# Spreading sums of squares by a block-of-ones matmul, with one full-width Abs_reciprocal_sqrt pass and the norm's gain folded into two weights

## The chip, the cores and the metric

The kernel runs on one core of a Trainium2 chip. The metric is the time of one execution on the device in microseconds; less is better. Before the change it is 224.84 us, the median of two runs (224.73 and 224.95).

A core has five engines, each working through its own queue of instructions in order: TensorE (PE: matmuls; its weight loads, PEld, overlap them), VectorE (DVE), ScalarE (ACT), GpSimd (POOL) and SyncE (SP). POOL and SP here mostly issue transfers, which 16 DMA engines carry out. Matmul results go to PSUM, everything else lies in SBUF. Engines wait for each other by semaphores.

## The reference

Linear attention per head with an RMS norm over the 64 elements of a head, followed by an RWKV channel mix over the 512 columns that 8 heads make (8 batches, 576 rows each):

```python
def _attn_ref(q, k, v, g_norm):                    # (8, 8, 576, 64)
    kv = np.einsum('bhsd,bhse->bhde', k, v)
    out = np.einsum('bhsd,bhde->bhse', q, kv)
    rms = np.sqrt(np.mean(out * out, axis=-1, keepdims=True) + 1e-06)
    return (out / rms * g_norm).astype(np.float32)

def _moe_ref(x, mu_k, mu_r, w_k, w_v, w_r):        # x: (8, 576, 512)
    x_prev = np.concatenate([np.zeros((B, 1, D)), x[:, :-1, :]], axis=1)
    xk = mu_k * x + (1.0 - mu_k) * x_prev
    xr = mu_r * x + (1.0 - mu_r) * x_prev
    k = np.maximum(xk @ w_k, 0.0)                  # w_k: (512, 1024)
    v = k * k @ w_v                                # w_v: (1024, 512)
    r = 1.0 / (1.0 + np.exp(-(xr @ w_r)))          # w_r: (512, 512)
    return (r * v).astype(np.float32)
```

The gain `g_norm` has 64 elements, the same for every head.

## The kernel before, in words

**Layout.** Heads are taken in pairs, so that a pair fills 128 partitions (64 rows of one head, 64 of the other): 4 pairs per batch. q, k and v come from memory as float32 and are cast to bf16 by the loading DMA, one transfer of 590 KB for each of them and each batch, all issued by POOL (L294) in one queue; batch 0 is loaded in three parts. The weights (L283) are in the same queue: w_r and w_k behind batch 0, w_v behind batch 1.

**Attention of one batch** (`attention_part`), by piece name:
- `kv`: 48 small matmuls k^T v (L361), copied to SBUF by ACT or DVE (`kv copy`).
- `qT`: q transposed, on PE with copies out of PSUM (L391) for batches 0 to 3, by a DMA transpose from SP (L380) for batches 4 to 7.
- `u`: four matmuls per pair (L411), copied to uT by ACT or DVE (`u copy`), then squared on DVE (`u sq`, L420).
- `st`: 16 matmuls per batch against `sel`, a table of single ones (L440), which collect the sums of squares in few PSUM rows, packed so that 144 columns hold all pairs. ACT takes Ln and then Exp with factor -0.5 over these 144 columns (`rs`, L445 and L446): 1/rms.
- `rr`: 16 matmuls per batch of `selg` with `rs` (L463), which spread 1/rms back to a head's 64 rows, in PSUM.
- `x`: DVE forms uT times g (a column of `mu_sb`) times the spread 1/rms (L471), reading uT from SBUF and the factor from PSUM.
- `d`, `t`, `xk`, `xr`: shifted differences and the two blends (L488 to L507), written to rings that hold four batches.

**The mix** works on groups g of 512 rows, nine in all, whose borders are not those of the batches (576 rows). Each has K (32 matmuls of 512 columns, L548, with relu on ACT and its square on DVE), R (16, L571, sigmoid on ACT) and V (32, L591, times the sigmoid on DVE, then stores from SP). V of one group uses the squares of its own K.

**What sets the order.** Nothing at run time. The class `Planner` takes pieces with an engine (or a choice of two), an assumed duration, dependencies, buffers of rings of fixed depth and a due time, plays a schedule, and emits the instructions of each engine in the order found. Ring depths matter here: two buffers each of k, v, q, qT, kv, uT; two PSUM buffers of each of the kinds `at` (attention) and `mm` (mix). A load (`load k 3`) is emitted for POOL once the buffer of two batches before is done with: k and v after that batch's `kv`, q after its `qT`. The planner prices a 590 KB load at 0.36 us times 8 heads. It fills PE's planned gaps with dummy matmuls on zeros (L620), up to a planned time of 80 us. Changing any duration can change every order.

Act tables: sigmoid needs one set of ScalarE tables, Ln and Exp another (`ln_table`, L228); each change is one load of 1.28 us in the trace.

Of the kernel before, what the change touches and what calls it, by code (L numbers as in the profile page):

```python
# [8 lines left out]
FP32 = mybir.dt.float32  # L9
BF16 = mybir.dt.bfloat16  # L10
AF = mybir.ActivationFunctionType
ALU = mybir.AluOpType
# [24 lines left out]
class Planner:  # L37
# [40 lines left out]
    def run(self, warm=None):  # L78


        free, order, queue, dma, modes = {}, [], [], 0.0, {"PE": None, "ACT": "ln"}
        while self.left:
            best = {}
            for p in self.left:
# [14 lines left out]
                _, t, eng = min(ways)  # L99
# [51 lines left out]
def kernel(  # L151
# [13 lines left out]
    nc = tc.nc  # L165

    B, H, S, HD = q.shape
# [4 lines left out]
    NJ = 6  # L172
    NP = S // NJ
    HS = S // 2
    SEC = S // 4
    NI = NJ // 2
    G = 512
    NG = B * S // G
# [16 lines left out]
        "ln": (2, (128, SEC), FP32),  # L195
        "rs": (2, (128, SEC), BF16),
# [28 lines left out]

    table = [None]

    def ln_table():  # L228
        if table[0] != "ln":
            nc.scalar.preload_act_table_set("natural_log_exp_and_others")  # L230
            table[0] = "ln"


    ident = const.tile([128, 128], BF16, name="ident")
# [5 lines left out]
    eps = const.tile([128, 1], FP32, name="eps")  # L240
    zeros = const.tile([128, 512], BF16, name="zeros")
    sel = const.tile([128, NHP, 32], BF16, name="sel")
    selg = const.tile([128, NHP, NHP, 2, HD], BF16, name="selg")
# [6 lines left out]

    def consts_small(_):
        nc.vector.memset(zeros, 0.0)
        nc.vector.memset(eps, 1e-6)
        ln_table()
# [5 lines left out]
        nc.vector.memset(sel, 0.0)  # L260
        for e in range(2):
            for s in range(NHP):
                nc.vector.memset(sel[64 * e:64 * e + 64, s, 2 * s + e:2 * s + e + 1], 1.0)

    def consts_idents(_):
        make_identity(nc, ident)
# [6 lines left out]
        nc.tensor.matmul(ps, mu_raw, ident9, start=True, stop=True)  # L273
        nc.vector.tensor_copy(out=mu_sb, in_=ps)

    def consts_selg(_):

        for tl in range(NHP):
            rows = ident[:, 32 * tl:32 * tl + 2 * NHP].rearrange("p (s e) -> p s e", e=2)
            nc.scalar.copy(out=selg[:, tl], in_=rows.unsqueeze(3).broadcast_to([128, NHP, 2, HD]))  # L280

    def load_w(dst, src):
        nc.gpsimd.dma_start(out=dst, in_=src.rearrange("(c p) n -> p c n", p=128))  # L283
# [8 lines left out]
    def load(b, n, h0, h1, due):  # L292
        def fn(_):
            nc.gpsimd.dma_start(  # L294
                out=get(kvq[(n, b)])[:, h0:h1, :],
                in_=src[n][b, h0:h1].rearrange("h (p j) d -> p h (j d)", j=NJ),
            )

        p = add(f"load {n} {b}", {"POOL": 0.8}, fn, bufs=[kvq[(n, b)]], due=due, land=(h1 - h0) * 0.36)
        for h in range(h0, h1):  # L300
            loaded[(n, b, h)] = p
# [10 lines left out]
    p_selg = add("selg", {"ACT": 2.4}, consts_selg, deps=[p_ident], due=-800)  # L312
    p_wr = add("load w_r", {"POOL": 0.8}, lambda _: load_w(w_r_sb, moe_w_r), due=-700, land=2.6)
    p_wk = add("load w_k", {"POOL": 0.8}, lambda _: load_w(w_k_sb, moe_w_k), due=-699, land=5.2)
    for n in ("k", "v", "q"):
        load(1, n, 0, H, -698)
    p_wv = add("load w_v", {"POOL": 0.8}, lambda _: load_w(w_v_sb, moe_w_v), due=-697, land=5.2)
    for b in range(2, B):
        for n in ("k", "v", "q"):
# [19 lines left out]
    def attention_part(b, part, bufs, ps_buf):  # L339
# [5 lines left out]
        ln, rs = Buf("ln"), Buf("rs")  # L345

        def due(x):
            return 20 * b - 2 * x - 4 if b else -100 - x
# [79 lines left out]
                           due=due(20)))  # L428


        def place(i, s):
            return NHP // n * i + s // n, s % n

        pst = ps_buf()

        def st_mm(_):
            for s in range(NHP):
                for i, hp in enumerate(hps):
                    tl, sub = place(i, s)
                    nc.tensor.matmul(get(pst)[32 * tl:32 * tl + 32, 0, 0:SEC], sel[:, sub],  # L440
                                     sq.t[:, hp, SEC * s:SEC * s + SEC], start=(sub == 0), stop=(sub == n - 1))

        def st_ln(_):
            ln_table()
            nc.scalar.activation(out=get(ln), in_=pst.t[:, 0, 0:SEC], func=AF.Ln, bias=eps, scale=1.0 / HD)  # L445
            nc.scalar.activation(out=get(rs), in_=ln.t, func=AF.Exp, scale=-0.5)  # L446

        m = add(f"st {b}", {"PE": 0.3}, st_mm, mode=2, deps=sqs, bufs=[pst, sq, ln, rs], due=due(18))
        st = add(f"rs {b}", {"ACT": 0.74}, st_ln, deps=[m], bufs=[pst, ln, rs], due=due(17), mode="ln")


        xms = []
        step = min(2, n)
        for hp1 in range(hp0, hp0 + n, step):
            for half in range(2):
                cs = slice(HS * half, HS * half + HS)
                xs = slice(NP + HS * half, NP + HS * half + HS)

                def rr_mm(_, hp1, half, ps):
                    for i in range(step):  # L460
                        for c in range(2):
                            tl, sub = place(hp1 - hp0 + i, 2 * half + c)
                            nc.tensor.matmul(get(ps)[:, i, SEC * c:SEC * c + SEC],  # L463
                                             selg[:, tl, sub].rearrange("p e d -> p (e d)"), rs.t,
                                             start=True, stop=True)

                def x_mul(_, hp1, cs, xs, ps):
                    if xT.t is None:
                        nc.vector.memset(get(xT)[:, :, 0:1], 0.0)
                    hs = slice(hp1, hp1 + step)  # L470
                    nc.vector.scalar_tensor_tensor(  # L471
                        out=xT.t[:, hs, xs], in0=get(uT)[:, hs].rearrange("q h i jj p -> q h (i jj p)")[:, :, cs],
                        scalar=g_col, in1=ps.t[:, 0:step, 0:HS], op0=ALU.mult, op1=ALU.mult)

                ps = ps_buf()
                m = add(f"rr {b}", {"PE": 0.13 * step}, lambda _, hp1=hp1, half=half, ps=ps: rr_mm(_, hp1, half, ps),
                        deps=[st, p_selg], bufs=[ps, rs, xT], due=due(14))
                xms.append(add(f"x {b}", {"DVE": 0.15 + 0.3 * step},
                               lambda _, hp1=hp1, cs=cs, xs=xs, ps=ps: x_mul(_, hp1, cs, xs, ps),
                               deps=[m, p_mu] + [us[hp1 + i] for i in range(step)], bufs=[ps, uT, xT],  # L480
                               due=due(13)))
        last_rr[b] = m


# [43 lines left out]
            row += cnt  # L528


    p_first = add("first", {"PE": 0.01}, lambda _: None, deps=x_ready[0]["r"] + [p_wr], bufs=[warm], due=-1)
    hold = add("hold", {"PE": 0.01}, lambda _: None, bufs=[warm], due=-2000)

    def mix(g):
# [23 lines left out]
        for f2 in range(NFC // 2):  # L558
            ps, rt, u = Buf("mm"), Buf("relu"), k0 + 2 * f2
            ms = []  # L560
            for x in range(2):
                ms.append(add(f"K {g}", {"PE": 0.865}, lambda _, fc=2 * f2 + x, ps=ps: k_mm(_, fc, ps),
                              deps=ms or need["k"] + [p_wk], bufs=[ps, sqk], due=u + x))
            a = add(f"relu {g}", {"ACT": 1.04}, lambda _, ps=ps, rt=rt: k_relu(_, ps, rt), deps=ms[1:], bufs=[ps, rt], due=u + 2)
            sqs.append(add(f"sqk {g}", {"DVE": 0.7}, lambda _, f2=f2, rt=rt: k_sq(_, f2, rt), deps=[a], bufs=[rt, sqk], due=u + 4))

# [86 lines left out]
```

## Time and profile before

| | us |
|---|---|
| median of the runs | 224.84 |
| span of the profiled execution | 222.2 |
| PE busy in it | 205.6 |
| of which K, V and R (L548, L591, L571) | 165.9 |
| of which dummy matmuls L620 | 15.3 |
| VectorE busy | 144.8 |
| ScalarE busy | 124.1 |
| DMA engines full until about | 111 |
| last matmul ends | 218.0 |

The groups that the change touches (line, engine, operation, output<-inputs, shapes, count, then busy us and mean ns of one, then the idle time of the engine before them and its releaser):

```profile
L471 DVE SCALAR_TENSOR_TENSOR xT<-uT,mu_sb,at 128x576 bf16<-128x576 bf16 x29 | 22.6, 810 | 3.0 <-PE at L463 2.7
L420 DVE TENSOR_TENSOR sq<-uT 128x576 bf16<-128x576 bf16 x32 | 13.3, 454 | 0.8 <-ACT uT L221 0.7
L463 PE MATMUL at<-rs,selg 128*128 128x144 bf16 x120 | 11.1, 226 | 0.7 <-DVE xT L471 0.7
L440 PE MATMUL at<-sq,sel 128*32 128x144 bf16 x128 | 3.8, 229 | 0.2
L445 ACT ACTIVATE ln<-at,eps 128x144 f32<-128x144 f32 x10 | 3.8, 379 | 5.5 <-PE at L440 5.4
L446 ACT ACTIVATE rs<-ln 128x144 bf16<-128x144 f32 x10 | 3.2, 323 | 0.3
```

How to read it: the busy time of a group is the time in which at least one of its instructions was under way; matmuls overlap, so 120 of 226 ns fill only 11.1 us. The idle time behind the last bar is that of the engine just before the group, with what ended it.

### The profile page before, as it was taken

Reading aid. Unit: us, or ns where it says so; the run is one execution under the profiler, and the core shown is the slowest. Engines: PE = TensorE matmul, PEld = TensorE weight load, DVE = VectorE, ACT = ScalarE, POOL = GpSimd, SP = SyncE. Lnnn points to the kernel's source line nnn. Section 1 sums busy time; section 2 is a strip of 40 time slices with the busy share of each in tenths; the row PEclk is TensorE's granted clock in tenths of the full one; section 3 lists DMA queues with packets and bytes.
Section 4 is the critical chain, followed back from the end, with each engine's and each line's share of the span. In section 5 each row is a group of like instructions: output and inputs, shape, how many; then the busy total and the mean of one; then the engine's idle time right before and its main releaser. Section 6 shows DMA issues by size and latency. Waiting matters only on the chain.

```text
span 222.2 us, 4055 instructions
## 1 busy us (share of the span) xinstructions
PE 205.6 (93%) x1671; PEld 102.5 (46%) x1671; DVE 144.8 (65%) x253; ACT 124.1 (56%) x172; POOL 25.8 (12%) x39
## 2 busy tenths in 40 slices
PE   2989999798799989999999999999999999999971
PEld 1445454455354444545454694445444444444430
DVE  1159857358989999899679869976963143143131
ACT  5367647725948929776678277847716306405500
POOL 7861031210300500400000000000000000000000
PEclk9999999999999999999999999999999999999999
DMA  5999999999999999999950420051033033033033
GB/s 74 190 201 208 203 207 203 203 205 244 204 203 157 229 173 191 197 211 191 188 158 3 106 86 0 0 152 39 0 98 90 3 96 96 0 86 105 0 94 94
DMA packets 36150, 28.84 MB, mean 130 GB/s; under 512 B 11036, under 2 KB 31012, under 8 KB 36132
## 3 DMA queue, kind: packets, MB, share of 16 engines
q0 software_dynamic: 21008, 16.78, 49.3%
q1 hardware_dynamic: 15124, 11.81, 23.9%
q8 instruction: 13, 0.21, 0.4%
q14 instruction: 5, 0.04, 0.0%
HBM read 33.56 MB, written 9.44 MB: 193 GB/s over the span
## 4 chain that ended last, share of the span: by engine, by line
PE 71%; DMA 18%; DVE 6%; POOL 1%; issue 1%; ACT 0%; DVEq 0%; POOLq 0%
PE mm L591 27%; PE mm L548 22%; DMA q<-in_q_dram 13%; PE mm L571 11%; DMA qT<-q 6%; PE at L463 3%; PE mm L620 2%; PE at L411 2%; PE at L361 1%; DVE xT L471 1%; DVE out L595 1%; PE at L391 1%; PE at L440 1%; POOL k L294 1%; DVE sq L420 1%
## 5 line engine op out<-in xcount | busy, mean ns | idle before, releaser
L591 PE MATMUL mm<-w_v,sqk 128*128 128x512 bf16 x288 | 65.7, 379 | 1.7 <-DVE out L595 1.7
L548 PE MATMUL mm<-xk,w_k 128*128 128x512 bf16 (+1 forms) x320 | 66.1, 358 | 1.0 <-DVE xk L507 1.0
L552 ACT ACTIVATE relu<-mm 128x1024 bf16<-128x1024 f32 x36 | 36.7, 1024 | 44.5 <-PE mm L548 42.8
L548 PEld LDWEIGHTS <-w_k 128*128 128x128 bf16 x320 | 30.3, 98 | 29.6 <-issue 1.7
L591 PEld LDWEIGHTS <-sqk 128*128 128x128 bf16 x288 | 27.2, 98 | 34.1 <-issue 3.6
L555 DVE TENSOR_TENSOR sqk<-relu 128x1024 bf16<-128x1024 bf16 x36 | 24.7, 689 | 24.1 <-ACT relu L552 24.1
L595 DVE TENSOR_TENSOR out<-mm,sig 128x1024 f32<-128x1024 f32 (+1 forms) x20 | 22.1, 1116 | 24.9 <-PE mm L591 24.9
L571 PE MATMUL mm<-w_r,xr 128*128 128x512 bf16 x144 | 34.1, 379 | 0.0
L471 DVE SCALAR_TENSOR_TENSOR xT<-uT,mu_sb,at 128x576 bf16<-128x576 bf16 (+1 forms) x31 | 23.6, 791 | 3.0 <-PE at L463 2.7
L576 ACT ACTIVATE sig<-mm 128x1024 bf16<-128x1024 f32 x18 | 18.4, 1023 | 10.5 <-PE mm L571 10.4
L504 ACT ACTIVATE t<-d,mu_sb 128x576 bf16<-128x576 bf16 x30 | 21.0, 770 | 3.0 <-DVE xr L507 1.9
L571 PEld LDWEIGHTS <-xr 128*128 128x128 bf16 x144 | 13.3, 98 | 14.2
L221 ACT CAST uT<-at 128x576 bf16<-128x576 f32 x19 | 11.7, 637 | 9.4 <-PE at L411 9.4
L620 PE MATMUL mm<-zeros 128*128 128x512 bf16 x52 | 15.3, 423 | 0.0
L420 DVE TENSOR_TENSOR sq<-uT 128x576 bf16<-128x576 bf16 x32 | 13.3, 454 | 0.8 <-ACT uT L221 0.7
L294 POOL DMA_DIRECT2D k<-in_k_dram x10 | 7.5, 750 | 42.7 <-PE at L361 40.1
L463 PEld LDWEIGHTS <-selg 128*128 128x128 bf16 x128 | 9.6, 98 | 6.2 <-issue 1.2
L463 PE MATMUL at<-rs,selg 128*128 128x144 bf16 x120 | 11.1, 226 | 0.7 <-DVE xT L471 0.7
L507 DVE TENSOR_TENSOR xk<-t,xT 128x2304 bf16<-128x2304 bf16 (+2 forms) x10 | 11.2, 1118 | 0.4
L489 DVE TENSOR_TENSOR d<-xT 128x2304 bf16<-128x2304 bf16 (+2 forms) x10 | 11.2, 1119 | 0.3
L507 DVE TENSOR_TENSOR xr<-t,xT 128x2304 bf16<-128x2304 bf16 (+2 forms) x10 | 11.0, 1112 | 0.0
L502 DVE TENSOR_SCALAR t<-d,mu_sb 128x576 bf16<-128x576 bf16 x34 | 10.4, 368 | 0.2
(51 smaller groups left out, 133.1 us busy)
## 6 DMA issues: line engine op xcount, KB each, us to landing
out_dram<-out SPq DMA_DIRECT2D x24, 192.0 KB, 2.5
k<-in_k_dram POOLq DMA_DIRECT2D x7, 576.0 KB, 14.6
v<-in_v_dram POOLq DMA_DIRECT2D x7, 576.0 KB, 16.8
q<-in_q_dram POOLq DMA_DIRECT2D x7, 576.0 KB, 16.4
out_dram<-out SPq DMA_DIRECT2D x24, 128.0 KB, 2.4
out_dram<-out SPq DMA_DIRECT2D x24, 64.0 KB, 2.0
w_k<-in_moe_w_k_dram POOLq DMA_DIRECT2D x1, 1024.0 KB, 12.9
w_v<-in_moe_w_v_dram POOLq DMA_DIRECT2D x1, 1024.0 KB, 23.5
```

Of the source, the lines that this page charges most:

```text
L463: nc.tensor.matmul(get(ps)[:, i, SEC * c:SEC * c + SEC], selg[:, tl, sub].rearrange("p e d -> p (e d)"), rs.t, start=True, stop=True)
L471: nc.vector.scalar_tensor_tensor(out=xT.t[:, hs, xs], in0=get(uT)[:, hs].rearrange("q h i jj p -> q h (i jj p)")[:, :, cs], scalar=g_col, ...
L504: nc.scalar.mul(out=dst, in_=d.t[:, hp, :], mul=by)
L507: nc.vector.tensor_tensor(out=dst[:, hsl, c0:c0 + S], in0=t.t[:, 0:n, :], in1=xT.t[:, hsl, 0:S], op=ALU.add)
L548: nc.tensor.matmul(get(ps)[:, fc % 2, a0:a1], w_k_sb[:, cc, 128 * fc:128 * fc + 128], xk[:, cc, x0:x0 + a1 - a0], start=(cc == 0), stop=(c ...
L552: nc.scalar.activation(out=get(rt), in_=ps.t, func=AF.Relu)
L555: nc.vector.tensor_mul(out=get(sqk)[:, 2 * f2:2 * f2 + 2, :], in0=rt.t, in1=rt.t)
L571: nc.tensor.matmul(get(ps)[:, ci % 2, :], xr[:, cc, n0:n0 + 128], w_r_sb[:, cc, :], start=(cc == 0), stop=(cc == NHP - 1))
L576: nc.scalar.activation(out=get(sg), in_=ps.t, func=AF.Sigmoid)
L591: nc.tensor.matmul(get(ps)[:, ci % 2, :], sqk.t[:, fc, 128 * ci:128 * ci + 128], w_v_sb[:, fc, :], start=(fc == 0), stop=(fc == NFC - 1))
L595: nc.vector.tensor_mul(out=get(ot)[:, xs, :], in0=ps.t[:, xs, :], in1=sg.t[:, xs, :])
L620: nc.tensor.matmul(get(buf or warm)[:, 0, :], zeros[:, 0:128], zeros, start=True, stop=True)
```

## The change

The sums of squares are now formed and spread in one step: `ones` has two blocks of 64x64 ones on its diagonal, so that a matmul of it with the squares of a pair gives, on every one of a head's 64 rows, the sum over that head. That is two matmuls of 288 columns per pair (`ss`), in place of `st` and `rr`. ACT then makes 1/rms for the whole pair (128x576) in one Abs_reciprocal_sqrt pass with the mean's factor and the epsilon in it, written to SBUF as bf16 (`rs`, now one per pair). `x` is a plain product of two bf16 SBUF tiles. The gain no longer enters there: w_r and w_k are multiplied in place by g, row by row, on DVE, once they have landed (`g w_r`, `g w_k`), and R's first matmul and K's first matmul wait for that. `sel`, `selg` and the tile of epsilons go. The planner is given durations for the new pieces.

```diff
-    def consts_selg(_):
-        for tl in range(NHP):
-            rows = ident[:, 32 * tl:32 * tl + 2 * NHP].rearrange("p (s e) -> p s e", e=2)
-            nc.scalar.copy(out=selg[:, tl], in_=rows.unsqueeze(3).broadcast_to([128, NHP, 2, HD]))
+    def by_g(w):
+        nc.vector.tensor_scalar_mul(out=w, in0=w, scalar1=g_col)
...
+        nc.vector.memset(ones, 0.0)
         for e in range(2):
+            nc.vector.memset(ones[64 * e:64 * e + 64, e, :], 1.0)
...
+    p_gr = add("g w_r", {"DVE": 0.65}, lambda _: by_g(w_r_sb), deps=[p_wr, p_mu], due=-50)
+    p_gk = add("g w_k", {"DVE": 1.2}, lambda _: by_g(w_k_sb), deps=[p_wk, p_mu], due=-2)
...
-        m = add(f"st {b}", {"PE": 0.3}, st_mm, mode=2, deps=sqs, bufs=[pst, sq, ln, rs], due=due(18))
-        st = add(f"rs {b}", {"ACT": 0.74}, st_ln, deps=[m], bufs=[pst, ln, rs], due=due(17), mode="ln")
...
-                m = add(f"rr {b}", {"PE": 0.13 * step}, lambda _, hp1=hp1, half=half, ps=ps: rr_mm(_, hp1, half, ps),
-                        deps=[st, p_selg], bufs=[ps, rs, xT], due=due(14))
-                xms.append(add(f"x {b}", {"DVE": 0.15 + 0.3 * step},
...
+        for i, hp in enumerate(hps):
+            rs, pss = Buf("rs"), ps_buf()
+            def ss_mm(_, hp, ps):
+                for half in range(2):
+                    nc.tensor.matmul(get(ps)[:, half, 0:HS], ones.rearrange("p e d -> p (e d)"),
+                                     sq.t[:, hp, HS * half:HS * half + HS], start=True, stop=True)
+            def ss_rs(_, rs, ps):
+                norm_table()
+                nc.scalar.activation(out=get(rs).rearrange("q (u c) -> q u c", c=HS), in_=ps.t[:, :, 0:HS],
+                                     func=AF.Abs_reciprocal_sqrt, bias=1e-6, scale=1.0 / HD)
+            def x_mul(_, hp, rs):
...
+                nc.vector.tensor_tensor(out=xT.t[:, hp, NP:NP + S], in0=flat(hp), in1=rs.t, op=ALU.mult)
+            m = add(f"ss {b}", {"PE": 0.25}, ..., deps=[sqs[i]], bufs=[pss, sq, rs], due=due(18))
+            st = add(f"rs {b}", {"ACT": 0.58}, ..., deps=[m], bufs=[pss, rs], due=due(17), mode="norm")
+            xms.append(add(f"x {b}", {"DVE": 0.38}, ..., deps=[st, us[hp]], bufs=[rs, uT, xT], due=due(13)))
...
-    p_first = add("first", {"PE": 0.01}, lambda _: None, deps=x_ready[0]["r"] + [p_wr], bufs=[warm], due=-1)
+    p_first = add("first", {"PE": 0.01}, lambda _: None, deps=x_ready[0]["r"] + [p_gr], bufs=[warm], due=-1)
...
-                              deps=ms or need["k"] + [p_wk], bufs=[ps, sqk], due=u + x))
+                              deps=ms or need["k"] + [p_gk], bufs=[ps, sqk], due=u + x))
```

The planner's starting act table is renamed from "ln" to "norm" with it, and `ln_table` becomes `norm_table`, which loads the set that holds Abs_reciprocal_sqrt.

More of the change, by code (lines that the diff above doesn't have):

```diff
@@ L78, in run @@
     def run(self, warm=None):
-        free, order, queue, dma, modes = {}, [], [], 0.0, {"PE": None, "ACT": "ln"}
+        free, order, queue, dma, modes = {}, [], [], 0.0, {"PE": None, "ACT": "norm"}
         while self.left:
@@ L174 @@
     HS = S // 2
-    SEC = S // 4
     NI = NJ // 2
@@ L194 @@
         "sq": (1, (128, NHP, S), BF16),
-        "ln": (2, (128, SEC), FP32),
-        "rs": (2, (128, SEC), BF16),
+        "rs": (2, (128, S), BF16),
         "xT": (2, (128, NHP, NP + S), BF16),
@@ L226, with norm_table @@
     table = [None]
[L228 to L231, printed above, removed]
+    def norm_table():
+        if table[0] != "norm":
+            nc.scalar.preload_act_table_set("abs_reciprocal_sqrt_and_small")
+            table[0] = "norm"
     ident = const.tile([128, 128], BF16, name="ident")
@@ L239 @@
     g_col = mu_sb[:, NM - 1:NM]
-    eps = const.tile([128, 1], FP32, name="eps")
     zeros = const.tile([128, 512], BF16, name="zeros")
-    sel = const.tile([128, NHP, 32], BF16, name="sel")
-    selg = const.tile([128, NHP, NHP, 2, HD], BF16, name="selg")
+    ones = const.tile([128, 2, HD], BF16, name="ones")
     w_r_sb = const.tile([128, NHP, C], BF16, name="w_r")
@@ L252, in consts_small @@
         nc.vector.memset(zeros, 0.0)
-        nc.vector.memset(eps, 1e-6)
-        ln_table()
+        norm_table()
         nc.sync.dma_start(out=mu_raw[0:NHP], in_=moe_mu_k.rearrange("(j p) -> j p", p=128))
@@ L258, in consts_small @@
             nc.sync.dma_start(out=mu_raw[NM - 1:NM, HD * e:HD * e + HD], in_=g_norm.rearrange("(o d) -> o d", o=1))
-        nc.vector.memset(sel, 0.0)
+        nc.vector.memset(ones, 0.0)
         for e in range(2):
-            for s in range(NHP):
-                nc.vector.memset(sel[64 * e:64 * e + 64, s, 2 * s + e:2 * s + e + 1], 1.0)
+            nc.vector.memset(ones[64 * e:64 * e + 64, e, :], 1.0)
     def consts_idents(_):
@@ L311 @@
     p_mu = add("mu", {"DVE": 0.5}, consts_mu, deps=[p_ident], bufs=[p_mu_ps], due=-800)
-    p_selg = add("selg", {"ACT": 2.4}, consts_selg, deps=[p_ident], due=-800)
     p_wr = add("load w_r", {"POOL": 0.8}, lambda _: load_w(w_r_sb, moe_w_r), due=-700, land=2.6)
@@ L344, in attention_part @@
         kv, qT, uT, sq, xT, d = (bufs[t] for t in ("kv", "qT", "uT", "sq", "xT", "d"))
-        ln, rs = Buf("ln"), Buf("rs")
         def due(x):
@@ L428, in attention_part @@
                            due=due(20)))
[L431 to L446, printed above, removed]
@@ L448, in attention_part @@
-        m = add(f"st {b}", {"PE": 0.3}, st_mm, mode=2, deps=sqs, bufs=[pst, sq, ln, rs], due=due(18))
-        st = add(f"rs {b}", {"ACT": 0.74}, st_ln, deps=[m], bufs=[pst, ln, rs], due=due(17), mode="ln")
-        xms = []
[L453 to L475, printed above, removed]
-                m = add(f"rr {b}", {"PE": 0.13 * step}, lambda _, hp1=hp1, half=half, ps=ps: rr_mm(_, hp1, half, ps),
-                        deps=[st, p_selg], bufs=[ps, rs, xT], due=due(14))
-                xms.append(add(f"x {b}", {"DVE": 0.15 + 0.3 * step},
-                               lambda _, hp1=hp1, cs=cs, xs=xs, ps=ps: x_mul(_, hp1, cs, xs, ps),
-                               deps=[m, p_mu] + [us[hp1 + i] for i in range(step)], bufs=[ps, uT, xT],
-                               due=due(13)))
@@ new lines, in attention_part @@
+        xms = []
+        for i, hp in enumerate(hps):
[5 more added lines that the diff above has]
+            def ss_rs(_, rs, ps):
+                norm_table()
+                nc.scalar.activation(out=get(rs).rearrange("q (u c) -> q u c", c=HS), in_=ps.t[:, :, 0:HS],
+                                     func=AF.Abs_reciprocal_sqrt, bias=1e-6, scale=1.0 / HD)
+            def x_mul(_, hp, rs):
+                if xT.t is None:
+                    nc.vector.memset(get(xT)[:, :, 0:1], 0.0)
+                nc.vector.tensor_tensor(out=xT.t[:, hp, NP:NP + S], in0=flat(hp), in1=rs.t, op=ALU.mult)
+            m = add(f"ss {b}", {"PE": 0.25}, lambda _, hp=hp, ps=pss: ss_mm(_, hp, ps), deps=[sqs[i]],
+                    bufs=[pss, sq, rs], due=due(18))
+            st = add(f"rs {b}", {"ACT": 0.58}, lambda _, rs=rs, ps=pss: ss_rs(_, rs, ps), deps=[m], bufs=[pss, rs],
+                     due=due(17), mode="norm")
+            xms.append(add(f"x {b}", {"DVE": 0.38}, lambda _, hp=hp, rs=rs: x_mul(_, hp, rs), deps=[st, us[hp]],
+                           bufs=[rs, uT, xT], due=due(13)))
```

## The prediction

> **What bounds the kernel now.** First the busy shares and slices of the page.
>
> ```profile
> PE 205.6 (93%) x1671; PEld 102.5 (46%) x1671; DVE 144.8 (65%) x253; ACT 124.1 (56%) x172; POOL 25.8 (12%) x39
> ...
> DMA  5999999999999999999950420051033033033033
> ```
>
> TensorE is busy almost throughout, but for the first half (20 slices of 5.6 us, to about 111 us) the DMA engines are full too. Next the stages, which give the engines' busy time in stretches of 10 us (PE, PEld, DVE, ACT, POOL, clock, DMA share, GB/s).
>
> ```profile
> 40.00:50.00 10.00, 8.65 (x123) 5.07 (x112) 4.80 (x9) 4.92 (x8) 2.30 (x3) 1.00 1.31 204
> 50.00:60.00 10.00, 7.56 (x108) 4.25 (x106) 9.21 (x17) 7.58 (x14) 1.53 (x2) 1.00 1.28 226
> 60.00:70.00 10.00, 9.99 (x86) 4.70 (x85) 8.96 (x16) 6.01 (x10) 0.77 (x1) 1.00 1.38 185
> ```
>
> Up to 60 us PE has holes (3.8 us in 40 to 60); from 60 us it is full. So before 60 us a microsecond of PE work may cost nothing, and after it costs a microsecond. PE's order of time shows what the holes wait for:
>
> ```profile
> 41.77 0.95 PE L361 MATMUL at<-v,k 96*64 96x64 bf16 x48 [1.22 <-DMA v<-in_v_dram]
> ...
> 54.17 0.95 PE L361 MATMUL at<-v,k 96*64 96x64 bf16 x48 [0.23 <-ACT uT L221]
> ...
> 56.90 1.46 PE L548 MATMUL mm<-xk,w_k 128*128 128x512 bf16 x6 [0.99 <-DVE xk L507]
> ```
>
> PE takes its queue in order: at 41.77 the k^T v product of batch 2 had to wait for v to land, with everything behind it. The chain of waits has two DMA links, the second being batch 4's q transposed by a DMA:
>
> ```profile
> 16.50 28.14 DMA q<-in_q_dram
> ...
> 63.59 12.60 DMA qT<-q
> ```
>
> Last, what the queues moved in two stretches, 56 to 66 us and 84 to 88 us (packets, MB; q0 carries the loads, q1 the transposes and stores):
>
> ```profile
> q0 software_dynamic: 2683, 2.02, 130.8%
> ...
> q0 software_dynamic: 759, 0.57, 90.8%
> q1 hardware_dynamic: 757, 0.19, 36.3%
> ```
>
> Loads alone move 202 KB/us, so a 590 KB load takes 2.9 us; beside a transpose 143, so 4.1 us, and the transpose gets 48, so a backlogged one takes 12.3 us.
>
> **What the Trainium skill says.** "DMA: Bandwidth & Descriptors", section "Queues, rings and completion order": each engine alternates between the queues it has work for, packet by packet. The trace agrees: 759 and 757 packets. "ScalarE: Activation LUTs", "What ACT_TABLE_LOAD costs": 186 ns + 0.833 ns per element with immediate scale and bias; the trace's relu of 1024 takes 1024 ns against 1039. "VectorE: DVE Perf Modes", "The perf-mode tier table": tensor_scalar on bf16 is a 4x operation, 693 ns for 2048; in the trace four t products of 576 take 1.22 us together, which fits. "TensorE: Matmul & The Clock Gate", "What's actually happening": PE falls to half clock after an idle window of about 3.4 us and needs a busy one to return. The trace shows only the start: six dummy matmuls in 2.67 us (445 ns each), against 216 ns in a warm run of four (0.86).
>
> **The change, part by part.**
> PE: out go 128 matmuls of L440 (0.36 us per batch) and 128 of L463 (four in 0.25, so 1.0). In come 64 of 128x288; at 216 ns per 512 columns, 0.12 each, 0.97 per batch. Net 0.39 per batch, 3.1 in all; batches 4 to 7 lie wholly in the full stretch: 1.6.
>
> VectorE: x was 25.3 us (L471, 22.6+1.0+0.9+0.8), all reading PSUM. Now 32 products of SBUF operands; the nearest row, sq at L420, has 454 ns: 14.5. So -10.8. The g products: w_r (2048) 0.7, w_k (4096) 1.2. The memsets change by 0.2. Net -9.
>
> ScalarE: out go Ln and Exp (3.8+3.2) and selg (2.2); in come 32 passes of 576 from PSUM. The skill's price is 0.67, the L221 copies of that shape 0.64: I take 0.65, 20.8 us. Range 0.58 (overlapped) to 0.74. The two builds' orders show 14 table loads against 12, at 1.28: +2.6. Net +14, on an engine that is 56% busy, hidden behind PE; uncovered it costs at most about a microsecond, where sig must free a mm buffer for V.
>
> New waits: R's first matmul waits for g w_r. That product stands in VectorE's queue before sq and x of batch 0's last heads and waits for w_r to land at about 17 us, holding them 0.5 to 0.8 us. The shorter x gives this back, and R begins 1 to 2 us before its 25.75. That is then lost: k^T v of batch 1 waits for v at 28.01 as before. K waits for g w_k, done near 25, long before K can start: nothing.
>
> POOL and SP issue the same transfers, but in another order: q5 before k5, and k7, v7 before q6. That follows from the step that matters. **The planner, given new durations, moves k^T v.** In the old order batch 4's stands inside R of group 1, batch 5's inside K of group 2. In the new order batch 4's directly follows batch 3's, **before K of group 1**; batch 5's is between K and R of group 1. The planner's own price per load, 0.36 x 8, is near the 2.9 measured, but it knows nothing of what stores and transposes take from loads.
>
> Follow PE in the new order:
> 1. q2 landed at 44.7 (PE's wait at 44.68). k3, v3, q3, k4, v4 follow without a gap: v4 lands at 44.7 + 5 x 2.92 = 59.3. Batch 3's product, after its q transposes (q3 at 53.4) and batch 2's ss, ends near 57.5: PE idles 1.8, runs batch 4's 0.88, starts K1 at 60.2 instead of 56.9.
> 2. K1 is 32 x 0.216 = 6.9; u and half of ss of batch 3 between take 1.3, their waits for ScalarE's copies and changes of shape about 1.9: PE reaches batch 5's product at 70.3.
> 3. q4 lands at 62.2, and SP issues its transpose at once. (Before, four stores issued from 48.89 came earlier and delayed this: 63.59.) Now those stores go out near 57 and take 1.4 from q5: 66.5. The transpose's packets start 3.9 us after issue, as they did at 67.5, so at 66.2. Then k5 crosses into the slow rate (323 KB left: 2.3, plus a 0.8 us pause that both transposes show), its data ending at 69.3; v5's takes 4.1, to 73.4, and lands 1.6 later: **75.0**. PE idles 4.7.
> 4. Product 0.88, R1 3.46, ss 0.5: 79.9. Then u of batch 4 wants the transpose: 66.2 + 12.3 + 0.8 + 0.9 = 80.2. Before, it had a thin load queue beside it and landed at 76.19.
> 5. Left after 80.2: V1 to V8 55.4, K2 to K8 48.5, R2 to R8 24.2, u4 to u7 3.0, ss4 to ss7 3.9, products 6 and 7 1.8: 136.8. The same sum over the old order from V1's start at 79.08 gives 135.7, where the last matmul ended at 217.97: 3.2 of waits and changes come on top. In the new order u of batch 6 stands four in a row with two PSUM buffers and ScalarE copies of 0.6: about 1 more. End 221.2, **+3.2**.
>
> The profiled span is 222.2, the median 224.84, 2.6 more. 222.2 + 3.2 + 2.6 = **228.0**.
>
> **The rivals.**
> A (likeliest), chance 0.50: as above, 226 to 229.5, the ends being v5 or the transpose 1.5 us earlier or later.
> B, slower, 0.32: the idle time at batch 5's product spans a whole clock window and PE resumes at half speed. It decides once the idle time passes 3.4 us; at 4.7 it depends on where the window falls, (4.7-3.4)/3.4 = 0.4. One to two windows at half speed cost 1.7 to 3.4 of work, say 2.4: 230.4, range 229 to 232. For it: matmuls of 445 ns at the start. Against it: no hole in the trace up to 200 us is that long.
> C, faster, 0.15: v5 lands before PE is there, because the stores or the transpose come later than I think or the pause is absent. Then PE is at u of batch 4 at 75.2 instead of 80.2, 5.0 less: 223.0; with the 1.8 before batch 4's product closed as well, 221.2. Against it: both waits must go, since the transpose alone still holds PE to 80.2.
> D, 0.03: ScalarE becomes the bound in a stage. At +1.7 us per batch of some 20 us it would be 8.5 of 10 in the fullest stage: 1 to 4 us, 229 to 232. A set lacking relu or copy would do it, but the build shows no load ahead of either.
>
> **The numbers.** The range 223.0 to 231.5 takes in A, the most of B and the upper part of C. Within 2%, about what a measurement of this kernel can tell from no change, is 220.3 to 229.3. Slower: most of B and D (0.31) and A's upper edge (0.07), 0.38. Faster: the far end of C, 0.04. Within: 0.58.
>
> **What would show it.** PE's product of batch 4 waits for v near 57.5 to 59.3, that of batch 5 near 70 to 75; K1 starts near 60; the transpose of batch 4 lands near 80; PE is full after that. rs takes 0.65, x 0.45, g w_r 0.7. If batch 5's product does not wait, C holds; if R1's matmuls stand 430 ns apart after it, B. A last matmul before 217 would make the forecast wrong.

## The result, and the profile after

The changed kernel takes **230.84 us** (median of two runs, 230.30 and 231.37) against 224.84 before: a ratio of 1.027 with an interval of 1.021 to 1.032. It is slower. The forecast was 228.0 with a range of 223.0 to 231.5. The traced run is the slower of the two, 231.37.

The span of the profiled execution grew from 222.2 to 229.2 us. The page's busy shares, and its rows of the granted clock and of the DMA engines in 40 slices:

```profile
PE 207.2 (90%) x1480; PEld 102.1 (45%) x1480; DVE 140.1 (61%) x259; ACT 127.2 (56%) x169; POOL 25.1 (11%) x39
...
PEclk9999999996599599999999999999999999999998
DMA  5999999999999999995810060024023023024033
```

TensorE issues about 190 matmuls fewer and is yet busy longer: in two places its clock falls to half, which the profile before never shows. The four stretches from 50 to 90 us (columns as in the prediction) hold what went wrong:

```profile
50.00:60.00 10.00, 7.28 (x113) 4.95 (x113) 9.28 (x19) 5.55 (x11) 1.70 (x3) 0.69 1.31 204
60.00:70.00 10.00, 9.23 (x80) 4.19 (x76) 8.77 (x17) 7.10 (x13) 2.16 (x3) 0.80 1.27 223
70.00:80.00 10.00, 5.93 (x65) 3.19 (x64) 4.13 (x10) 4.49 (x6) 1.53 (x2) 0.71 1.31 176
80.00:90.00 10.00, 10.00 (x57) 4.16 (x56) 6.23 (x12) 7.93 (x11) 0.77 (x1) 0.95 1.28 203
```

From 60 to 70 PE was full before; now it has a hole there, and from 70 to 80 it stands idle 4.1 us. PE's order of time (start, busy time, work; in brackets the wait and what ended it) says for what:

```profile
57.29 1.49 PE L352 MATMUL at<-v,k 96*64 96x64 bf16 x48
59.46 1.49 PE L352 MATMUL at<-v,k 96*64 96x64 bf16 x48 [0.68 <-DMA v<-in_v_dram]
60.88 1.89 PE L513 MATMUL mm<-xk,w_k 128*128 128x512 bf16 x4
...
67.43 4.48 PE L513 MATMUL mm<-xk,w_k 128*128 128x512 bf16 x20
75.98 1.49 PE L352 MATMUL at<-v,k 96*64 96x64 bf16 x48 [4.07 <-DMA v<-in_v_dram]
77.40 0.66 PE L428 MATMUL at<-sq,ones 128*128 128x288 bf16 x2
77.86 3.47 PE L536 MATMUL mm<-w_r,xr 128*128 128x512 bf16 x8
...
81.41 1.89 PE L536 MATMUL mm<-w_r,xr 128*128 128x512 bf16 x8
83.23 0.32 PE L402 MATMUL at<-qT,kv 64*64 64x288 bf16 x4
```

L352 is k^T v (L361 before): batches 3 and 4 follow each other, batch 4's waits for its v, then K of group 1 begins, and batch 5's product stands behind K and waits 4.07 us for its v. The first eight matmuls of R (L536) take 3.47 us, the next eight 1.89: half and full clock. Only at 83.23 does u of batch 4 (L402) begin, behind which V of group 1 stands. From that point to the end PE is nearly full, in both kernels. The chain of waits has the same transfer, v of batch 5, as its last DMA link, where the kernel before had the transposed q of batch 4:

```profile
59.84 16.10 DMA v<-in_v_dram
75.98 1.49 PE at L352 x26
```

The new operations themselves (columns as in the table of groups before):

```profile
L433 ACT ACTIVATE rs<-at 128x576 bf16<-128x576 f32 x29 | 18.0, 652 | 9.5 <-PE at L428 9.0
...
L439 DVE TENSOR_TENSOR xT<-uT,rs 128x576 bf16<-128x576 bf16 x32 | 14.2, 454 | 2.2 <-ACT rs L433 1.9
```

They cost what was expected of them, 652 and 454 ns.

### The profile page after: what moved, and what is told of

Its sections match the earlier page's. It is cut to its first block, busy times and chain, and to the rows that moved or that the text cites. A ratio compares the mean times of both kernels' runs of the same rounds, so it can differ in the third digit from the quotient of the medians.

```text
span 229.2 us, 3705 instructions
## 1 busy us (share of the span) xinstructions
PE 207.2 (90%) x1480; PEld 102.1 (45%) x1480; DVE 140.1 (61%) x259; ACT 127.2 (56%) x169; POOL 25.1 (11%) x39
## 4 chain that ended last, share of the span: by engine, by line
PE 66%; DMA 27%; DVE 2%; POOL 2%; issue 1%; ACT 1%; DVEq 0%; POOLq 0%
PE mm L556 25%; PE mm L513 22%; DMA q<-in_q_dram 20%; PE mm L536 13%; DMA v<-in_v_dram 7%; PE at L428 2%; PE at L352 2%; PE at L402 1%; PE at L382 1%; DVE out L560 1%; DVE uT L221 1%; POOL k L285 1%; POOL v L285 0%; POOL w_k L274 0%; ACT rs L433 0%
## 5 line engine op out<-in xcount | busy, mean ns | idle before, releaser
L513 PE MATMUL mm<-xk,w_k 128*128 128x512 bf16 (+1 forms) x320 | 67.3, 362 | 0.0
L536 PE MATMUL mm<-w_r,xr 128*128 128x512 bf16 x144 | 34.3, 392 | 0.0
L433 ACT ACTIVATE rs<-at 128x576 bf16<-128x576 f32 x29 | 18.0, 652 | 9.5 <-PE at L428 9.0
L536 PEld LDWEIGHTS <-xr 128*128 128x128 bf16 x144 | 14.4, 101 | 17.3 <-issue 1.7
L439 DVE TENSOR_TENSOR xT<-uT,rs 128x576 bf16<-128x576 bf16 x32 | 14.2, 454 | 2.2 <-ACT rs L433 1.9
L352 PE MATMUL at<-v,k 96*64 96x64 bf16 x360 | 9.0, 214 | 7.2 <-DMA v<-in_v_dram 6.6
L467 DVE TENSOR_SCALAR t<-d,mu_sb 128x576 bf16<-128x576 bf16 x50 | 15.4, 369 | 0.1
L219 ACT CAST kv<-at 64x256 bf16<-64x256 f32 (+1 forms) x26 | 8.9, 341 | 9.5 <-PE at L352 7.6
L352 PEld LDWEIGHTS <-k 96*64 96x64 bf16 x384 | 9.3, 131 | 10.4 <-issue 10.1
L221 DVE CAST uT<-at 128x576 bf16<-128x576 f32 x12 | 8.8, 754 | 6.0 <-PE at L402 5.9
L428 PE MATMUL at<-sq,ones 128*128 128x288 bf16 x58 | 11.6, 301 | 0.4 <-ACT uT L219 0.2
```

Of the source, the lines that this page charges most:

```text
L219: nc.scalar.copy(out=dst, in_=src)
L352: nc.tensor.matmul(get(pkv)[64 * e:64 * e + 64, 0, HD * i:HD * i + HD], kin.t[:, h, HD * j:HD * j + HD], vin.t[:, h, HD * j:HD * j + HD], ...
L428: nc.tensor.matmul(get(ps)[:, half, 0:HS], ones.rearrange("p e d -> p (e d)"), sq.t[:, hp, HS * half:HS * half + HS], start=True, stop=True)
L433: nc.scalar.activation(out=get(rs).rearrange("q (u c) -> q u c", c=HS), in_=ps.t[:, :, 0:HS], func=AF.Abs_reciprocal_sqrt, bias=1e-6, scal ...
L467: nc.vector.tensor_scalar_mul(out=dst, in0=d.t[:, hp, :], scalar1=by)
L513: nc.tensor.matmul(get(ps)[:, fc % 2, a0:a1], w_k_sb[:, cc, 128 * fc:128 * fc + 128], xk[:, cc, x0:x0 + a1 - a0], start=(cc == 0), stop=(c ...
```

## The experiments

Three theories stood at the start. *Order*: the arithmetic is harmless, and the time goes to the places that the planner gave to k^T v of batches 4 and 5, which meet late transfers. *Operations*: the new work, above all 32 ScalarE passes, makes the kernel slower wherever it stands. *Clock*: it is the half speed after the wait that costs, not the wait.

| run | kernel changed | us | ratio to before, interval | span, clock |
|---|---|---|---|---|
| m1 | after | 233.52 | 1.038, 1.034 to 1.042 | 231.8, 0.952 |
| m2 | after | 228.27 | 1.017, 1.010 to 1.023 | 224.6, 0.981 |
| m3 | after | 228.59 | 1.019, 1.014 to 1.025 | 225.3, 0.989 |
| m4 | after | 229.86 | 1.025, 1.021 to 1.028 | 227.6, 0.982 |
| m5 | before | 231.02 | 1.030, 1.028 to 1.033 | 229.0, 0.978 |
| d1 | after | 220.10 | 0.981, 0.980 to 0.983 | 217.9, 0.999 |
| **d2** | after | **217.28** | 0.968, 0.966 to 0.969 | 215.3, 0.999 |
| d3 | before | 225.46 | 1.005, 1.003 to 1.007 | 221.6, 0.995 |
| d4 | before | 230.90 | 1.030, 1.028 to 1.031 | 228.5, 0.983 |
| d5 | before | 242.76 | 1.082, 1.078 to 1.086 | 240.6, 0.973 |
| o1 | d2 | 223.91 | 0.997, 0.995 to 0.999 | 221.5, 0.988 |
| c1 | after | 230.21 | 1.027, 1.024 to 1.029 | 229.1, 0.980 |

The kernel before had a median of 224.4 to 224.5 beside each of them. Span and clock (the mean granted clock, 1 is full speed) are those of the traced run; for m2 and d3 that was one of the fastest (226.72 and 223.68). Of the times expected in advance, c1's range and m4's 229.5 came out (m4 to 0.4), and o1 fell between its two. Every other run was slower than the theory that it bears out had allowed, by 0.3 us (d2) to 14.8 (d5): the runs bear the theories out in direction at best, not in size.

**m1 to m3: pieces moved by hand.** A list of moves takes named pieces out of the planner's finished order and puts them ahead of the i-th piece of another name; nothing else changes.

```diff
+        for names, (anchor, i) in self.moves:
+            at = nth(anchor, i)
+            group = [p for p in order if isinstance(p, Piece) and p.name in names]
+            order = [p for p in order if p not in group]
+            n = order.index(at)
+            order[n:n] = group
...
+    plan.moves = [(['kv 5', 'kv copy 5', 'load k 7', 'load v 7'], ('u 4', 0))]
```

That is m1: batch 5's product goes behind R of group 1, so that R fills the wait for v.

> Only the order is changed: batch 5's k^T v product, its copies and the two loads that it releases stand behind R of group 1 instead of before it. Order theory (PE's queue stands behind transfers that come late): the wait for v of batch 5 (4.1 us) goes, but batch 4's transposed q, which landed at 81.9 in the changed kernel, is next, 4 to 5 us after PE comes to it, and the clock may fall again: 229.5 to 231.5, little or no gain. If v of batch 5 is the only wall: 226. Operations theory (the longer ScalarE passes and the g products cost the time): 230.8, as every operation stays.

PE's order of time in m1 (lines of this kernel are 9 higher):

```profile
76.70 0.95 PE L361 MATMUL at<-v,k 96*64 96x64 bf16 x48
82.08 0.46 PE L411 MATMUL at<-qT,kv 64*64 64x288 bf16 x4 [4.43 <-DMA qT<-q]
82.46 5.67 PE L565 MATMUL mm<-w_v,sqk 128*128 128x512 bf16 x16
```

The wait for v is gone, and a wait of 4.43 us for the transpose stands in its place; the clock falls there too (16 matmuls of V in 5.67 us, against 3.63 at full clock in m4), and once more near 128 us. So the idle time at 82 was bound twice, by v and by the transpose, as rival C said against itself. Why m1 is 2.7 us slower than the changed kernel is not settled; the third stretch at half clock, 3.4 us long, would account for 1.7 of it.

m2 takes u of batch 4 out of the way as well, behind five of the eight parts of V:

```diff
+    plan.moves = [(['kv 5', 'kv copy 5', 'load k 7', 'load v 7'], ('V 1', 0)),
+                  (['u 4', 'u copy 4', 'u sq 4'], ('V 1', 5))]
```

> Only the order is changed: as the run before, and u of batch 4 (matmuls, copies, squares) stands behind the first five pieces of V of group 1. Order theory: PE waits neither for v of batch 5 nor for batch 4's transpose, V of group 1 starts near 77.3 instead of 83.5 and the second drop of the clock is gone: 224.6, range 223.5 to 226.5. Operations theory: 230.8, unchanged. Clock theory (the half-speed stretches are the loss, the waits only their occasion): 2.4 us less, 228.4.

```profile
75.72 0.95 PE L361 MATMUL at<-v,k 96*64 96x64 bf16 x48 [0.38 <-DMA v<-in_v_dram]
76.60 4.73 PE L565 MATMUL mm<-w_v,sqk 128*128 128x512 bf16 x20
81.40 0.44 PE L411 MATMUL at<-qT,kv 64*64 64x288 bf16 x8
82.58 0.32 PE L411 MATMUL at<-qT,kv 64*64 64x288 bf16 x4 [0.73 <-ACT uT L228]
83.63 0.32 PE L411 MATMUL at<-qT,kv 64*64 64x288 bf16 x4 [0.74 <-ACT uT L228]
```

V of group 1 begins at 76.60 instead of 83.48, and the second fall of the clock is gone. The time falls by 2.6 us with every operation kept, and all four runs (226.72 to 229.49) lie below the two of the changed kernel: *operations* cannot be the whole cause. It does not reach the 224.5 of the kernel before. The four u matmul groups now stand together, and PE waits twice, 1.5 us in all, for ScalarE to empty a PSUM buffer; the rest is not accounted for.

m3 moves batch 4's product as well, to the end of K of group 1 (move added: `(['kv 4', 'kv copy 4', 'load k 6', 'load v 6'], ('K 1', -1))`).

> As the run before, and batch 4's k^T v product stands before the last piece of K of group 1 instead of ahead of all of K. Order theory: K of group 1 starts near 58.8 instead of 60.9, but what is behind it has been waiting for copies as well, so 0 to 2 us less than the run before: 223 to 225. Operations theory: 230.8.

K starts at 57.95 instead of 60.88, but then waits 1.00 and 1.42 us for relu, whose place in ScalarE's queue was not moved with it. Nothing is gained over m2. This trace comes up again under m5.

**m4: the clock kept up.** 19 matmuls on zeros ahead of batch 5's product fill the wait.

```diff
+            for _ in range(19 if b == 5 else 0):
+                nc.tensor.matmul(get(pkv)[:, 0, :], zeros[:, 0:128], zeros, start=True, stop=True)
```

> The changed kernel with 19 dummy matmuls on zeros (about 4.1 us) put ahead of batch 5's k^T v product, so that PE is not idle while it waits for v. Clock theory: the second half-speed stretch (74.2 to 81.0) is gone and with it 2.4 us: 228.4. Order theory: batch 4's transpose lands at 81.9 either way and PE then waits for that, so 1.3 us less at most: 229.5. If the clock falls for another reason than idle time: 230.8.

```profile
71.17 4.26 PE L358 MATMUL at<-zeros 128*128 128x512 bf16 x19
75.36 0.95 PE L363 MATMUL at<-v,k 96*64 96x64 bf16 x48
...
81.58 0.32 PE L413 MATMUL at<-qT,kv 64*64 64x288 bf16 x4 [1.22 <-DMA qT<-q]
```

The second fall is gone, R runs at full clock, and u begins only 1.65 us earlier than in the changed kernel (83.23), because it has to wait 1.22 us for the transpose. The medians lie 1.0 us apart (229.86 and 230.84, with overlapping intervals): the half clock at R is worth at most 1.65 us here, not the 2.4 that rival B gave it.

**m5: the old arithmetic with the products moved.** The counterpart: the kernel before, with batch 4's product moved ahead of the third part of K, batch 5's ahead of the last part of R. Its loads k5 and v5 keep their place ahead of q5, and its stores stay early.

```diff
+    plan.moves = [(['kv 4', 'kv copy 4', 'load k 6', 'load v 6'], ('K 1', 2)),
+                  (['kv 5', 'kv copy 5', 'load k 7', 'load v 7'], ('R 1', 3))]
```

> The kernel before with its old arithmetic, and k^T v of batch 4 moved ahead of the third part of K of group 1, that of batch 5 ahead of the last part of R of group 1; the loads of k5 and v5 keep their place ahead of q5. If the position of the products on PE is what costs, 227 to 229. If it is the position together with the order of the loads (q5 ahead of k5 and v5, stores late), v5 is there near 69 and the time stays at 224.5 to 226.5.

231.02 us: as slow as the changed kernel, without one new operation. Neither expectation had the size. The second was right that v comes in time, and the first that the position costs; what both lacked is where it costs. PE's order of time:

```profile
72.28 0.95 PE L370 MATMUL at<-v,k 96*64 96x64 bf16 x48
...
76.22 1.04 PE L557 MATMUL mm<-xk,w_k 128*128 128x512 bf16 x4
82.10 0.45 PE L420 MATMUL at<-qT,kv 64*64 64x288 bf16 x4 [4.84 <-DMA qT<-q]
```

The transpose of batch 4 was issued at 63.54 here and at 63.59 in the kernel before, but it landed about 82.1 instead of 76.19. What the queues moved (packets, MB, share) from 72 to 76 us in the kernel before:

```profile
q1 hardware_dynamic: 1856, 0.64, 101.9%
q0 software_dynamic: 217, 0.15, 24.7%
```

and from 74 to 78 in m5:

```profile
q0 software_dynamic: 701, 0.53, 106.0%
q1 hardware_dynamic: 710, 0.18, 52.9%
```

Before, the load queue (q0) had little left by 72, for batch 4's product had not yet released k and v, and POOL issued k6 at 72.90; the transposing queue then had the engines almost alone. In m5 the product is done by 61.6, POOL issues k6 and v6 from 62.46, and the two queues share packet for packet until the transpose is done (from 72 to 76 us too: 748 and 749 packets). In the changed kernel k6 and v6 are issued at 61.82 and 62.59.

m2 and m3 show the same in the new arithmetic, the other way round. They differ in batch 4's product alone, with its copies and the loads that it releases: k6 is issued at 61.72 in m2 and at 70.55 in m3. The transpose is issued at 63.54 and 63.61, and POOL's load that waits for it goes out at 81.92 and 77.19. From 72 to 76 us the queues of m2 share (q0 618 packets, q1 619); in m3:

```profile
q1 hardware_dynamic: 1545, 0.58, 85.7%
q0 software_dynamic: 322, 0.24, 38.9%
```

In m3 nothing used the 4.7 us, for u of batch 4 stood behind V. **A product moved ahead releases two loads that delay the transpose which its own batch needs next.** A run that moves the product and holds the loads back was not made.

**d1 and d2: the planner told to be later.** If the order is at fault, it should be mendable without touching the arithmetic. d1 changes one number in the changed kernel, the due time of the attention of batches 1 to 7, by 14 us; d2 changes three prices as well (two of PE's, and the landing time assumed for the transposes).

```diff
-            return 20 * b - 2 * x - 4 if b else -100 - x
+            return 20 * b - 2 * x + 10 if b else -100 - x
... (d2 only:)
-    LAT = {"PE": 0.25, "ACT": 0.15, "DVE": 0.12, "POOL": 0.15, "SP": 0.0}
+    LAT = {"PE": 0.1, "ACT": 0.15, "DVE": 0.12, "POOL": 0.15, "SP": 0.0}
-    SLACK = {"PE": 0.0}
+    SLACK = {"PE": 0.05}
-            m = add(f"qT dma {b}", {"SP": 7.8}, q_dma, ..., land=3.5)
+            m = add(f"qT dma {b}", {"SP": 7.8}, q_dma, ..., land=7)
```

> The changed kernel with one number changed: the planner's due times of all attention pieces of batches 1 to 7 are 14 later, so that K, R and V go first and batches 4 and 5 are begun when their loads have landed. Order theory: no wait for v of batch 5 or for batch 4's transpose, no second drop of the clock; counted from the matmuls left and the holes that remain, 6 to 8 us under the kernel before: 216 to 219. Operations theory: 228 to 231, since all operations stay.

> As the run before, with three more of the planner's prices nearer to what the trace shows: PE to another engine 0.10 instead of 0.25, a slack of 0.05 on PE's starts, the transposing DMA 7 instead of 3.5. Order theory: the holes left in the order of the run before (some 3 us between 45 and 200 us) nearly vanish: 1 to 3 us less than it, 214 to 217. Operations theory: 228 to 231.

220.10 and 217.28 us, with every operation of the changed kernel: both faster than the kernel before, d1 by 1.9% and d2 by 3.2%, though neither quite reaches its expected range. d2 is the fastest kernel of this study. Its page, and PE's order of time around the products of batches 4 and 5:

```profile
PE 200.9 (93%) x1476; PEld 97.7 (45%) x1476; DVE 144.6 (67%) x271; ACT 120.0 (56%) x157; POOL 25.4 (12%) x39
...
PEclk9999999999999999999999999999999999999999
```

```profile
56.20 1.89 PE L513 MATMUL mm<-xk,w_k 128*128 128x512 bf16 x8
...
77.22 0.95 PE L352 MATMUL at<-v,k 96*64 96x64 bf16 x48
...
97.40 0.95 PE L352 MATMUL at<-v,k 96*64 96x64 bf16 x48
```

K of group 1 starts at 56.20, the products of batches 4 and 5 come at 77.22 and 97.40, wait for nothing, and the clock never falls. k6 is issued at 79.04.

**d3 to d5: the same freedom for the old arithmetic.** Is d2 fast by its order alone? d4 and d5 give the kernel before exactly the numbers of d2 and of d1. d3 has the three prices and due times 20 later.

> The kernel before, old arithmetic, given the same kind of order: due times 20 later (14 leaves it with large holes, so each arithmetic gets the shift that suits it) and the same three prices. If the new arithmetic is worth something by itself, 4 to 6 us more than the run before, that is 1 to 4 us under the kernel before: 221 to 223.5. If only the order matters, the same time as the run before, 214 to 217.

> The kernel before, with exactly the four planner numbers of d2 (due times 14 later, two PE prices, landing price of the transposes). If the gain of d2 came from the planner's numbers alone, 216 to 219. If the new arithmetic carries it (fewer pieces and PSUM passes between a batch's u and its x), this stays at 223 to 227, as d3 with 20 in place of 14 did at 225.5, with waits of PE for VectorE.

> The kernel before with the one number of d1 alone (due times 14 later). Numbers alone: 219 to 221.5, as d1. New arithmetic needed: 223 to 228.

225.46, 230.90 and 242.76: none beats the kernel before. What the waits of PE are, in the list of waits of d5 (us, times, longest):

```profile
PE mm L548 <- DVE xk L507: 12.1, 7, 3.3
```

In d4 it is 3.4 us in 4 waits, the longest 1.9.

With the attention late, K waits for xk, the last product of the chain from u over the squares, the sums, 1/rms, x, d and t. In the old arithmetic that chain has one more PE pass and PSUM reads at 810 ns in place of SBUF reads at 454; the new one bears the lateness: PE's waits in d1 and d2 hold none for xk or xr. With the same four numbers, the new arithmetic is 13.6 us faster (d2 against d4), but these numbers had been chosen for it; between the best orders found for each it is 7.1 us (217.28 against 224.4, the kernel before itself). Five orders run are no proof that the old arithmetic has no better one.

**o1: what ScalarE's passes cost.** d2 with each Abs_reciprocal_sqrt pass issued twice into the same tile.

```diff
+                for _ in range(2):
+                    nc.scalar.activation(out=get(rs)..., func=AF.Abs_reciprocal_sqrt, bias=1e-6, scale=1.0 / HD)
```

> The second run of this set with every Abs_reciprocal_sqrt pass issued twice on the same data (the planner's order is the same). Operations theory: the longer passes are what costs, so 32 more of 0.57 to 0.65 us bring 10 to 20 us. Order theory: ScalarE has room, as it is under 60% busy: 0 to 3 us, where a pass delays x or a sigmoid that PE waits for.

It costs 6.6 us, between the two theories. Stretches of d2 (PE, PEld, DVE, ACT, POOL, clock, DMA share, GB/s):

```profile
0.00:65.00 65.00, 56.59 (x540) 28.41 (x540) 43.75 (x95) 42.96 (x68) 20.67 (x33) 1.00 1.20 197
65.00:130.00 65.00, 65.00 (x513) 33.20 (x512) 56.05 (x105) 41.07 (x51) 4.72 (x6) 1.00 0.95 164
130.00:200.00 70.00, 70.00 (x386) 32.21 (x384) 41.58 (x69) 33.89 (x38) 0.00 (x0) 1.00 0.22 61
```

and of o1:

```profile
0.00:65.00 65.00, 52.66 (x486) 25.98 (x488) 39.10 (x86) 46.02 (x72) 18.98 (x31) 0.97 1.18 194
65.00:130.00 65.00, 64.48 (x539) 33.45 (x534) 54.59 (x101) 48.41 (x66) 6.27 (x8) 1.00 1.06 168
130.00:200.00 70.00, 69.78 (x395) 31.62 (x394) 45.33 (x78) 40.06 (x47) 0.00 (x0) 1.00 0.19 53
```

From 65 us on ACT takes 7.3 and 6.2 us more, and PE loses 0.5 and 0.2. Before 65, PE loses 3.9, and a stretch at half clock adds to it: the product of batch 3 comes at 64.65 instead of 59.40. (The two runs of o1 at full clock throughout took 222.44 and 222.83, so some 5.3 us are left without it.) So a second pass on ScalarE is hidden where PE is full, and not in the first 65 us, where it stands in the chain that PE waits for. That is d2's order; what the single pass costs in the changed kernel was not run.

**c1: why the clock fell at 53.7.** Five matmuls on zeros ahead of the second pair of block-of-ones matmuls of batch 2, behind which PE stood idle 0.9 us.

```diff
+                for _ in range(5 if b == 2 and hp == hps[1] else 0):
+                    nc.tensor.matmul(get(ps)[:, 0, :], zeros[:, 0:128], zeros, start=True, stop=True)
```

> The kernel after with five dummy matmuls on zeros ahead of the second pair of block-of-ones matmuls of batch 2, where PE stands idle 0.9 us for q of batch 3 before the clock falls at 53.8. If the clock falls for too little PE work in some 3.4 us, the stretch at half clock from 53.8 on goes; if it falls for another reason, it stays. The time should hardly change either way, 229 to 231.5, since v of batch 5 (75.9) and the transpose of batch 4 (81.9) still hold PE; should it fall to 228 or less, the first drop cost more than I read from the trace.

PE's stretch ahead of the fall (busy, matmuls, clock, DMA share, GB/s), in the changed kernel and in c1:

```profile
50.30:53.70 3.40, 1.78 (x19) 1.00 1.31 203
```

```profile
50.30:53.70 3.40, 2.68 (x19) 1.00 1.31 203
```

With PE busy 79% of it instead of 52%, the clock does not fall at 53.7. It falls at 59.6, during the wait for batch 4's v, and for 3.4 us instead of 10.2. How much of this the filling did, one trace can't say. m1 to m4 leave this stretch as it is in the changed kernel, and their clocks fall at 55.9, 55.6, 56.4 and 55.7, for 10.2, 6.8, 3.4 and 6.8 us. That all five traces without the filling fall by 56.4 and c1's does not speaks for it; the shorter stretch does not, for m3 has it too.

The time is 230.21, as expected no gain that can be told: PE reaches the wait for batch 5's v 0.2 us earlier, v lands 0.7 later, and the wait is 4.93 us instead of 4.07. What the first fall costs stays open.

## Why the prediction was right, and where it was off

**The order: right, and shown.** The planner put batch 4's product ahead of K, batch 5's between K and R. Expected, and measured in the trace after: K starts at 60.2 / 60.9; v of batch 5 lands at 75.0 / 75.9; PE idles for it 4.7 / 4.1; the transpose lands at 80.2 / about 81.9, where POOL's q load that waits for it goes out (81.94). d1 and d2 remove the loss with the new arithmetic; m5 has one as large with the old, but at the transpose alone. Its v comes in time, so the wait for v needs, besides the product's place, something that m5 left as it was: its loads k5 and v5 ahead of q5 and its early stores, or the earlier product of batch 3 that releases them. Which of these, no run parts.

**The price of each operation: right.** rs 0.652 us against 0.65, x 0.454 against 0.454, g on w_r 0.755 against 0.7, on w_k 1.28 against 1.2. The sums of the engines were not: VectorE came to 140.1 (-4.7, expected -9), ScalarE to 127.2 (+3.1, expected +14). The planner chose engines anew: VectorE took 50 of the t products, 15.4 us against 10.4 before, off ScalarE. It is in neither of the sums that set the forecast's end.

**The 2.8 us that the likeliest number was short: step 4.** "Within 2%" was held likelier (0.58) than slower (0.38), and slower it is. Step 4 had R at full clock, and u of batch 4 at 80.2, the landing of the transpose. u began at 83.23, 3.0 later. The transpose itself was 1.7 late, and R, half of it at half clock, ended at 83.2. m4 parts the two: with the clock kept, u still began only at 81.58. So rival B happened, and its place was right; its price was not, because the transpose covers a part of it. That its 230.4 is so near is luck: it gave the clock 2.4 us, which is at most 1.65, and it had the transpose on time, which accounts for the other 1.4. Its rule was wrong too: it let the fall begin after 3.4 us of idle time, but the clock fell at 74.2, after 2.3. The first fall, at 53.7, stands in no step and no rival.

**Step 5: right in its sum.** From u of batch 4 to the last matmul the prediction has 141.0 us (221.2 - 80.2); the trace has 141.7 (224.92 - 83.23). The waits at u of batch 6 that it named are there, 1.4 us together (0.74 and 0.35 in u, 0.35 in the product behind it), each for a copy of uT, but on VectorE and not on ScalarE. The 2.6 us between span and median was 1.6 this time, and half of that 1.0 is only that the slower run was traced. On the trace the forecast was short by 3.7. Together: 3.0 + 0.7 - 1.0 = 2.7 of the 2.8.

**Rivals.** C fails as its own counter-argument said: m1 takes v's wait away, and the transpose takes its place. D does not show: even from 90 to 100 us, where ScalarE is busy 9.14 of 10 us, PE is full (10.00). But "hidden behind PE" was too broad a statement. By o1 it holds from 65 us on and not before.

**The change's worth was out of the prediction's reach.** It gave the change 1.6 us on PE in the full stretch and -9 on VectorE, and treated the order as given. It is worth more, 7 us against the best old order that was run, but only in an order in which the attention may be late. Of the 6.9 us by which d2's span is shorter than that of the kernel before, PE's busy time has 4.7 (205.6 to 200.9) and its idle time 2.2. How much of this the shorter chain from u to x gives was not run by itself; that the old arithmetic waits for xk in the late order and the new does not is what speaks for it. No step of the prediction asked for that.

**Open.** Whether a planner with true prices for transfers would find an order better than d2 was not tried, nor what the g products cost by themselves. How the 6 us divide between the wait for v, the late transpose and the two stretches at half clock is bounded only in part (m1, m2 and m4).

## What to carry to other kernels

In a kernel whose order comes from a planner, a new duration is a new order on every queue: compare the orders first, and look for the place where an in-order queue meets a transfer that is still under way. Work moved ahead also releases buffers ahead, and the loads that this starts take bandwidth from the transfer that is needed next. Before an arithmetic change is judged by its time, give the planner's due times a few other values: here the same arithmetic ran in 230.8 and in 217.3 us.

## What the runs showed of the hardware that was not expected

The clock falls without an idle window. The Trainium skill, "TensorE: Matmul & The Clock Gate", "What's actually happening", has PE go cold after at least one idle window of some 3.4 us. These traces differ: it fell after 3.4 us with PE busy 1.78 (at 53.7), 1.16 (at 74.2) and, in c1, 2.06 (at 59.6). The lengths at half clock agree with the page's window of 3413 ns: 10.2 us (53.7 to 64.0), 6.8 (74.2 to 81.0) and, in c1, 3.4 (59.6 to 63.0).

The changes keep a beat. Within a trace they lie whole multiples of 3.41 us apart: at 53.74, 63.98, 74.22 and 81.05 in the changed kernel (3, 6 and 8 beats after the first), at 55.93, 66.17, 79.82, 86.65, 127.61 and 131.02 in m1 (3, 7, 9, 21 and 22). The beat lies differently in each trace, so what a hole costs depends on where it falls. c1's clock stayed full through 3.4 us in which PE did nothing (71.8 to 75.2) and fell at 76.6, five beats after 59.56.

PE's busy time does not decide alone, even between two beats: m3's clock fell after 2.17 us of 3.41 (52.96 to 56.37), and d5's, which has its first fall at 97.75 and 27 beats later is at 189.90, did not after 1.54 (189.90 to 193.31). What else counts is not shown.

A transpose by DMA takes 12.6 us from issue when the load queue runs dry halfway (before, 63.59 to 76.19; 13.6 in m3), and over 18 when it does not (63.30 to 81.9 in the changed kernel, 63.54 to 82.1 in m5).
